# A hand-ordered attention and softplus-MLP kernel: a new order of all steps, a start without filler transposes, wider products in seven sweeps, and another DRAM layout for parked activations

## The chip, the cores and the metric

The kernel runs on one core of one Trainium2 chip. The metric is the device time of one execution in microseconds (us), as the median of several runs. One further execution was recorded by the hardware profiler; all rows below come from it.

## The reference

```python
def _attn_ref(x, state):                      # x: 8,8,512,64   state: 8,8,32,64
    scores = scale * x @ state^T ; a = softmax(scores) ; xread = a @ state
    scores2 = scale * state @ x^T ; a2 = softmax(scores2) ; sread = a2 @ x
    return concat([xread, sread], axis=2)     # 8,8,544,64
...
def _moe_ref(x, w_in, w_out):                 # x: 4352 x 512 after the heads are merged
    h = x @ w_in                              # 512 -> 2048
    g = max(h, 0) + log1p(exp(-abs(h)))       # softplus
    return (g @ w_out).astype(float32)        # 2048 -> 512
```

The weights arrive in double precision and are converted on the chip. Every large float32 product is made of three products of rounded halves (high by high, high by low, low by high): `PASSES`.

## The kernel before, in words

The eight batches are worked on as stages of one long list. For batch b, `B.Q` makes the scores (bank `sc`), a softmax follows on VectorE and ScalarE, `B.V` multiplies the state with the first weight (`V.b.c.g`), and `h.b.f` (16 of them per batch, six matmuls of 512 columns each) gives a 128-wide slice of the hidden layer in one PSUM bank. ScalarE takes the softplus (`s.b...`, line 719 or 646). `B.K` makes the same first-weight products for batches 4 to 7 together, parked in DRAM (`vd`). `B.R` and `T` make the read of x by the state (`rp`, `tp`); they need `Lx` and `Le` loads from DRAM (`in_xn`, `te`).

Batch 0 takes its second product in the plain form (`m.0.f.c`, bank `acc`, 12 matmuls of 512 columns for each f). Batches 1 to 7 park the softplus of each pair u of slices in DRAM (`Td.b.u`, tile `td`, 512 KB) and fetch it again for each half of the rows (`Tr.b.s.u`, 256 KB). The second product then runs in sweeps z = b.s, and one sweep 8.0 for the state rows: for each of 8 units u, VectorE forms sums and differences of four blocks (`sfa`, `sfb`, `sfc`, lines 744 to 747), ScalarE and VectorE split them into high and low halves (`gh`, `gl`, lines 312 and 328), and TensorE makes seven products of 256 columns in place of eight (a Winograd form). They collect in four banks X, Y, Z and Q over the sweep: steps `p.z.u.0` to `p.z.u.3`. A sweep ends with `e1` to `e6`, additions on VectorE (line 773) and one copy on ScalarE (line 776), which empty the banks into `ev`, and the stores `So`.

A product is three matmuls of 256 columns (line 766): low and high halves of the weight are two right-hand sides. Product 6 (bank Q) is in the wide form: the high half of g meets both halves of the weight in one matmul of 512 columns (line 762), the low half of g meets the high half of the weight in one of 256 (line 763). The bank then holds two parts, and the sweep's end adds both (`e6l`, `e6`). The last sweep, 7.1, has five banks and no wide product.

The order is written out by hand: `PLAN` is one list of steps, `name:engine:places`. The letter is T for TensorE, V and W for VectorE, A and C for ScalarE, S for the SyncE (SP) queue that issues the DMAs. C and W are the other way to convert a weight, with a plain copy (line 365) in place of the one on line 363 and two VectorE operations for one. The numbers behind a name are places in SBUF or PSUM; a step waits for the last user of its place. Each engine works through its steps in the order of the list, so a step that waits holds up all that stand behind it on its engine. Steps `w.i` are fillers: two 128x128 transposes into a bank that nobody reads (`wp`).

Of the kernel before, what the change touches and what calls it, by code (L numbers as in the profile page):

```python
# [56 lines left out]
Lk.0:S:23 Nm.1.1:V: D.1.0:T:5 cfa.0:V:24 Lk.1:S: cfa.1:V:25 m.0.2.2:T: cfb.0:V: cfb.1:V: wh.3:A:26 vl.1.0.1:V: gh.0.3:A:28 wl.3:V: Wh.0:A: Wh.1:A: gl.0.3:V:
ah.1.0:A:42 Wl.0:V: ah.0.0:A:32 w.4:T:2 w.5:T:2 w.6:T:2 w.7:T:2 w.8:T:2 w.9:T:2 w.10:T:2 w.11:T:2 m.0.3.3:T: Wl.1:V: ah.0.1:A:34 al.1.0:V: D.1.1:T:2 Lo.4:S:38
ch.2.1:C:87 cu.1.0:V:30 m.0.3.1:T: cu.1.1:V: ah.1.1:A:44 E.0.1:V: m.0.3.0:T: o.0.0.3:A:58 m.0.3.2:T: al.1.1:V: o.0.0.1:A:22 ch.2.0:C:93 Lo.5:S:74 cr.1.0:V:
h.1.0:T:1 o.0.0.0:A:67 cu.1.3:V:54 Li.3.0:S:46 cr.1.1:V: o.0.0.2:A:66 h.1.2:T:4 ch.2.2:C:95 cr.1.3:V: Sf.1.0:S: uh.0.2:A:36 cu.1.2:V: Li.3.1:S:78 al.0.0:V:  # L60
# [900 lines left out]
```

## Time and profile before

| what | value |
|---|---|
| median of 3 runs | 630.94 us (630.7 to 631.95) |
| the profiled execution's own time | 633.1 us |
| its span, first to last instruction | 631.3 us |
| TensorE, VectorE, ScalarE busy | 98%, 80%, 63% |
| DMA, mean rate over the span | 223 GB/s |

Matmuls are pipelined: a matmul's shown duration is longer than the distance to the next one, so the pace of a series is read from the starts, and a TensorE that is shown busy can still be idle for a moment. Idle time that the timeline prints in brackets is a gap that no modelled end covers, with what ended it.

### The profile page before, as it was taken

Reading aid. Unit: us, or ns where it says so; the run is one execution under the profiler, and the core shown is the slowest. Engines: PE = TensorE matmul, PEld = TensorE weight load, DVE = VectorE, ACT = ScalarE, POOL = GpSimd, SP = SyncE. Lnnn points to the kernel's source line nnn. Section 1 sums busy time; section 2 is a strip of 40 time slices with the busy share of each in tenths; the row PEclk is TensorE's granted clock in tenths of the full one; section 3 lists DMA queues with packets and bytes.
Section 4 is the critical chain, followed back from the end, with each engine's and each line's share of the span. In section 5 each row is a group of like instructions: output and inputs, shape, how many; then the busy total and the mean of one; then the engine's idle time right before and its main releaser. Section 6 shows DMA issues by size and latency. Waiting matters only on the chain.

```text
span 631.3 us, 12414 instructions
## 1 busy us (share of the span) xinstructions
PE 617.0 (98%) x4604; PEld 530.2 (84%) x4604; DVE 504.0 (80%) x1081; ACT 397.2 (63%) x659; POOL 1.0 (0%) x7
## 2 busy tenths in 40 slices
PE   8999999999999999999999999999999999999997
PEld 5576766577889988888988899899999999999997
DVE  3899688678999679885969988897975877878973
ACT  3899689999955448583736664576643454546440
POOL 0000000000000000000000000000000000000000
PEclk9999999999999999999999999999999999999999
DMA  9969766669906669968799857863848574431411
GB/s 343 415 226 327 289 232 240 255 231 399 353 19 216 193 200 254 294 206 281 241 294 319 255 189 257 266 224 124 288 128 271 208 246 141 138 107 33 152 51 35
DMA packets 64253, 141.07 MB, mean 223 GB/s; under 512 B 7360, under 2 KB 17600, under 8 KB 64192
## 3 DMA queue, kind: packets, MB, share of 16 engines
q1 hardware_dynamic: 63904, 139.62, 65.6%
q8 instruction: 36, 0.59, 0.4%
q10 hardware_dynamic: 288, 0.66, 0.3%
q14 instruction: 25, 0.20, 0.1%
HBM read 83.10 MB, written 57.15 MB: 222 GB/s over the span
## 4 chain that ended last, share of the span: by engine, by line
PE 70%; DVE 14%; DMA 10%; issue 2%; ACT 2%; SPq 2%; DVEq 0%; ACTq 0%
PE h L331 21%; PE pk_X L766 9%; PE pk_Y L766 9%; PE pk_Z L766 9%; PE acc L331 7%; DVE arena L328 4%; DMA arena<-td 3%; PE pk_Q L762 3%; PE h L820 2%; PE vp L331 2%; DMA arena<-vd 2%; PE vq L331 2%; SPq L319 1%; DVE arena L744 1%; PE pk_Q L763 1%
## 5 line engine op out<-in xcount | busy, mean ns | idle before, releaser
L312 ACT CAST arena<-arena 128x512 fp32r<-128x512 f32 (+2 forms) x255 | 185.8, 763 | 140.2 <-DVE arena L747 46.5
L328 DVE TENSOR_TENSOR arena<-arena,arena 128x512 fp32r<-128x512 f32 (+2 forms) x255 | 213.5, 858 | 58.3 <-ACT arena L312 56.1
L331 PE MATMUL h<-arena,arena 128*128 128x512 f32 x760 | 190.3, 399 | 0.0
L331 PEld LDWEIGHTS h<-arena,arena 128*128 128x128 f32 x760 | 138.3, 188 | 40.0 <-issue 4.2
L766 PE MATMUL pk_Y<-arena,arena 128*128 128x256 f32 x720 | 106.2, 284 | 0.4 <-DVE arena L328 0.4
L766 PE MATMUL pk_X<-arena,arena 128*128 128x256 f32 x720 | 105.5, 283 | 0.0
L766 PE MATMUL pk_Z<-arena,arena 128*128 128x256 f32 x696 | 103.8, 284 | 0.4 <-DVE arena L328 0.4
L766 PEld LDWEIGHTS pk_X<-arena,arena 128*128 128x128 f32 x720 | 96.6, 189 | 5.9
L766 PEld LDWEIGHTS pk_Y<-arena,arena 128*128 128x128 f32 x720 | 94.9, 190 | 1.1 <-DVE arena L328 0.6
L766 PEld LDWEIGHTS pk_Z<-arena,arena 128*128 128x128 f32 x696 | 92.2, 191 | 1.8 <-issue 0.8
L719 ACT ACTIVATE arena<-h 128x512 f32<-128x512 f32 x112 | 66.6, 613 | 29.8 <-PE h L331 25.7
L744 DVE TENSOR_TENSOR arena<-arena 128x256 f32<-128x256 f32 x120 | 49.5, 419 | 25.0 <-DMA arena<-td 23.9
L331 PE MATMUL acc<-arena,arena 128*128 128x512 f32 x192 | 45.7, 396 | 0.0
L762 PE MATMUL pk_Q<-arena,arena 128*128 128x512 f32 x112 | 44.8, 401 | 0.0
L331 PEld LDWEIGHTS acc<-arena,arena 128*128 128x128 f32 x192 | 35.8, 188 | 8.1 <-issue 1.0
L747 DVE TENSOR_TENSOR arena<-arena 128x128 f32<-128x128 f32 x120 | 33.6, 287 | 1.7
L746 DVE TENSOR_TENSOR arena<-arena 128x128 f32<-128x128 f32 x120 | 33.4, 287 | 1.4
L763 PE MATMUL pk_Q<-arena,arena 128*128 128x256 f32 x112 | 31.4, 280 | 0.0
L820 PE MATMUL h<-sreadT,arena 128*128 128x512 f32 x64 | 22.8, 393 | 0.0
L762 PEld LDWEIGHTS pk_Q<-arena,arena 128*128 128x128 f32 x112 | 21.3, 190 | 1.3 <-issue 0.8
L378 DVE SCALAR_TENSOR_TENSOR arena<-arena,arena 128x512 int32<-128x512 int32 x31 | 21.0, 688 | 0.5
L763 PEld LDWEIGHTS pk_Q<-arena,arena 128*128 128x128 f32 x112 | 21.3, 190 | 0.0
(99 smaller groups left out, 548.2 us busy)
## 6 DMA issues: line engine op xcount, KB each, us to landing
td<-arena SPq DMA_DIRECT2D x56, 512.0 KB, 4.3
arena<-td SPq DMA_DIRECT2D x112, 256.0 KB, 4.4
arena<-in_w_in_dram SPq DMA_DIRECT2D x16, 512.0 KB, 8.6
arena<-in_w_out_dram SPq DMA_DIRECT2D x16, 512.0 KB, 7.5
vd<-arena SPq DMA_DIRECT2D x32, 256.0 KB, 2.9
arena<-vd SPq DMA_DIRECT2D x64, 128.0 KB, 4.3
arena<-in_xn_dram SPq DMA_DIRECT2D x16, 512.0 KB, 6.4
arena<-in_xt_dram SPq DMA_DIRECT2D x15, 512.0 KB, 6.5
```

What stands on the lines that cost most here:

```text
L312: nc.scalar.copy(dst, src)
L328: lambda e: eng(e).tensor_tensor(r(dlo()), src(), dhi(), ALU.subtract))
L331: nc.tensor.matmul(dst, lhs, rhs, start=start, stop=stop)
L378: nc.vector.scalar_tensor_tensor(u, h2().bitcast(I32), 3, u, ALU.logical_shift_left, ALU.bitwise_or)
L719: nc.scalar.activation(t[:, :, 0::3] if i == 0 else t[:, :, 1:3], src.rearrange("p (s c t) -> p s c t", s=2, t=P), AF.Softplus)
L744: op(f"sfa.{k}", "V", t, [f"t.{k}:a"], lambda e, g=blocks: nc.vector.tensor_tensor(g()[:, 0:2], g()[:, 4:7:2], g()[:, 7:8].broadcast_to([P ...
L746: op(f"sfb.{k}", "V", [t[0], f"t.{k}:a"], [f"t.{k}:b"], lambda e, g=blocks: nc.vector.tensor_tensor(g()[:, 2], g()[:, 1], g()[:, 4], ALU.add))
L747: op(f"sfc.{k}", "V", [t[1], f"t.{k}:b"], [f"t.{k}:c"], lambda e, g=blocks: nc.vector.tensor_tensor(g()[:, 3], g()[:, 5], g()[:, 2], ALU.s ...
L762: nc.tensor.matmul(at(bank), g(0), r(wform(u, m)(slice(0, 2))), start=first, stop=False, skip_group_check=True)
L763: nc.tensor.matmul(at(bank)[:, 0:256], g(1), r(wform(u, m)(0)), start=False, stop=True, skip_group_check=True)
L766: nc.tensor.matmul(at(bank)[:, 256 * half:256 * half + 256], g(gi), r(wform(u, m)(wi)), start=first and pi == ps[0] and i == 0, stop=i == ...
L820: nc.tensor.matmul(hb, r(w[:, 0, cs]), r(at("sreadT")[:, :, kt, :]), start=kt == 0, stop=False, skip_group_check=True)
```

## The change

Four things, made together.

- `WIDE` names seven sweeps (4.1, 5.0, 5.1, 6.0, 6.1, 7.0 and 8.0) in which products 4, 5 and 6 take the wide form. Products 4 and 5 (bank Z before) then need a bank each, Z and W, so that a unit has five steps (`p.z.u.4` is new) and the sweep five banks; its end has four additions of 256 columns (`e5l`, `e5`, `e7l`, `e7`) in place of one of 512 (`e5`).
- Of the 14 filler steps, `w.1` to `w.13` are gone. `ch.o3` and `cu.o3`, and two more pairs, move from one conversion form to the other.
- The order of all steps is new. TensorE's own order is nearly the same up to the sweeps; moved are mainly `B.R0` to `B.R3`, `B.Q6`, `B.Q7`, the `T` steps and some `h` steps. VectorE's, ScalarE's and SP's orders, and many places, are new throughout.
- `td` is two solid blocks for each pair of slices, one for each half of the rows; the store writes two runs of 2 KB per partition in place of one of 4 KB, and a fetch reads one solid block of 256 KB.

In the token that guards the overwriting of half of a weight (`used`), the name is new and the steps it stands for are the same.

```diff
-WIDE = {}
+WIDE = {(4, 1): (4, 5, 6), (5, 0): (4, 5, 6), (5, 1): (4, 5, 6), (6, 0): (4, 5, 6), (6, 1): (4, 5, 6), (7, 0): (4, 5, 6), (8, 0): (4, 5, 6)}
...
-            used = [f"acc.{b}.{x}.{c}:{f1}" for b, x, f0, fe in RUNS if f0 <= f1 < fe for c in range(4)]
+            used = [f"W.{f1}:u{b}{c}" for b in PLAIN for c in range(4)]
...
-            op(f"m.{k}.{c}", "T", [...], [f"{acc}:{f}"], gemm2)
+            op(f"m.{k}.{c}", "T", [...], [f"{acc}:{f}", f"W.{f}:u{b}{c}"], gemm2)
...
-            store(f"Td.{b}.{u}", [...], lambda b=b, u=u: io.td[b, u], lambda b=b, u=u: at(f"tt.{b}.{u}"), [f"D:td.{b}.{u}"])
+            store(f"Td.{b}.{u}", [...], lambda b=b, u=u: io.td[b, u].rearrange("s p n -> p s n"), lambda b=b, u=u: at(f"tt.{b}.{u}").rearrange("p (s n) -> p s n", s=2), [f"D:td.{b}.{u}"])
...
-                     lambda b=b, s=s, u=u: io.td[b, u][:, 512 * s:512 * s + 512], [f"D:td.{b}.{u}"])
+                     lambda b=b, s=s, u=u: io.td[b, u][s], [f"D:td.{b}.{u}"])
...
-    io.td = {(b, u): dp.tile([P, 1024], F32, ...) ...}
+    io.td = {(b, u): dp.tile([2, P, 512], F32, ...) ...}
```

TensorE's order at the places that the prediction speaks of (unchanged neighbours cut):

```diff
-V.0.0.1.0 w.2 w.3 V.0.0.1.1 B.V1.0
+V.0.0.1.0 V.0.0.1.1 B.V1.0
...
-D.1.0 m.0.2.2 w.4 w.5 w.6 w.7 w.8 w.9 w.10 w.11 m.0.3.3 D.1.1 m.0.3.1 m.0.3.0 m.0.3.2 h.1.0
+D.1.0 m.0.2.2 m.0.3.3 D.1.1 m.0.3.1 m.0.3.0 m.0.3.2 h.1.0
...
-p.2.0.0.0 p.2.0.0.1 B.R4 h.4.12 p.2.0.0.2
+p.2.0.0.0 p.2.0.0.1 p.2.0.0.2 B.R4 p.2.0.1.1
...
-p.2.0.3.2 B.R0 p.2.0.3.3
+p.2.0.3.2 p.2.0.3.3 p.2.0.4.1 p.2.0.4.2 p.2.0.4.3 p.2.0.5.1 p.2.0.4.0 p.2.0.5.0 p.2.0.5.2 B.R0
...
-p.2.1.1.3 B.R1 h.5.3
+p.2.1.1.3 h.5.3 B.R1
...
-p.3.0.0.2 p.3.0.0.3 p.3.0.1.0 p.3.0.1.1 p.3.0.1.2 p.3.0.1.3 h.5.9 p.3.0.2.0 B.R2
+p.3.0.0.2 B.R2 p.3.0.0.3
...
-p.3.0.3.3 h.5.10 B.Q6 h.5.11 p.3.0.4.0
+p.3.0.3.3 h.5.10 h.5.11 p.3.0.4.1 p.3.0.4.2 p.3.0.4.0 B.Q6
...
-B.R3 h.5.15 T.3 T.5
+B.R3 p.3.1.4.2 T.3
```

ScalarE's and VectorE's order in the start, and SP's ahead of `Lz.3` and around `Le.2` and `Lz.6`:

```diff
-A: wh.2 ch.o3 m.1.0 m.1.1 ch.1.0 ch.1.1 ch.1.2 ch.1.3 s.0.3 wh.3 gh.0.3 Wh.0 Wh.1 ah.1.0
+A: wh.2 ch.o3 s.0.3 m.1.0 m.1.1 gh.0.3 wh.3 ch.1.0 ch.1.1 ah.1.0
-V: N.1.0 N.1.1 Nm.1.0 Nm.1.1 cfa.0 cfa.1 cfb.0 cfb.1 vl.1.0.1 wl.3 gl.0.3 Wl.0 Wl.1 al.1.0 cu.1.0 cu.1.1 E.0.1 al.1.1
+V: N.1.0 vl.1.0.1 Nm.1.0 gl.0.3 wl.3 N.1.1 Nm.1.1 cu.1.0 cu.1.1 al.1.0 cr.1.0 al.1.1
-S: Td.1.0 Sf.2.0 Td.1.1 Sf.2.1 Td.1.2 Lt.2.0 Lt.2.1 Lt.3.0 Lt.3.1 Td.1.3 Lz.2 Sf.3.0 Lz.3
+S: Lo.5 Lo.6 Sf.2.0 Sf.2.1 Lt.2.0 Lt.2.1 Lt.3.0 Lt.3.1 Td.1.2 Td.1.3 Lz.2 Td.1.0 Td.1.1 Sf.3.0 Sf.3.1 Lz.3
...
-S: Tr.3.0.2 Tr.3.0.3 Lx.2.0 Lx.2.1 Td.5.3 Le.2.0 Le.2.1 Le.2.2 Le.2.3
+S: Lx.2.0 Lx.2.1 Le.2.0 Le.2.1 Le.2.2 Le.2.3 Tr.3.0.2 Td.5.3 Tr.3.0.3
...
-S: So.2.1.0 Lt.6.0 So.2.1.1 Tr.3.0.4 Tr.3.0.5 Lt.6.1 Td.5.4 Tr.3.0.7 Lz.6
+S: So.2.1.0 Lz.6 So.2.1.1 Tr.3.0.6 Tr.3.0.4 Se.5.0 Se.5.1 Lq.3.1 Tr.3.0.5 Lt.6.0 Td.5.4 Lt.6.1 Lq.3.0 Tr.3.0.7
```

## Rows read from the trace of the kernel before

**Rows 1.** Page, part 1: busy time, share of the span, instructions of each engine.
```profile
PE 617.0 (98%) x4604; PEld 530.2 (84%) x4604; DVE 504.0 (80%) x1081; ACT 397.2 (63%) x659; POOL 1.0 (0%) x7
```
**Rows 2.** Busy time by stretch; the last three columns: granted clock, DMA share, GB/s.
```profile
20.00:44.00 24.00, 23.53 (x125) 14.90 (x124) 20.93 (x44) 21.44 (x38) 0.00 (x0) 1.00 0.84 325
44.00:100.00 56.00, 55.38 (x367) 37.68 (x366) 46.67 (x94) 48.41 (x87) 0.00 (x0) 1.00 0.77 275
...
240.00:360.00 120.00, 114.70 (x1134) 104.39 (x1133) 99.95 (x233) 76.61 (x119) 0.00 (x0) 1.00 0.87 271
...
430.00:620.00 190.00, 190.00 (x1429) 179.76 (x1428) 148.80 (x312) 91.53 (x147) 0.00 (x0) 1.00 0.47 153
```
**Rows 3.** Timeline of TensorE between 240 and 430: pieces with an idle gap.
```profile
253.41 1.10 PE L331 MATMUL rp<-arena,arena 128*32 128x64 f32 x64 [1.54 <-DMA td<-arena]
265.97 1.10 PE L331 MATMUL rp<-arena,arena 128*32 128x64 f32 x64 [0.21 <-issue]
281.39 0.74 PE L766 MATMUL pk_Y<-arena,arena 128*128 128x256 f32 x4 [0.37 <-DVE arena L328]
291.35 1.10 PE L331 MATMUL rp<-arena,arena 128*32 128x64 f32 x64 [1.01 <-DMA out_dram<-arena]
332.33 1.09 PE L331 MATMUL sc<-arena,arena 64*32 64x512 f32 x16 [2.06 <-DMA arena<-in_zp_dram]
361.41 0.44 PE L539 MATMUL tp<-ident,arena 128*128 128x128 f32 x2 [0.50 <-ACT arena L536]
```
**Rows 4.** Timeline of TensorE in the start: fillers and their neighbours.
```profile
22.32 0.94 PE L615 MATMUL wp<-ident 128*128 128x128 f32 x4
...
37.21 3.85 PE L615 MATMUL wp<-ident 128*128 128x128 f32 x16
40.82 0.94 PE L331 MATMUL acc<-arena,arena 128*128 128x512 f32 x3
```
**Rows 5.** Timeline of ScalarE in the start.
```profile
23.87 0.37 ACT L312 COPY arena<-vp 128x256 f32<-128x256 f32 x1 [0.66 <-PE vp L331]
...
30.02 1.28 ACT L363 ACT_TABLE_LOAD   x1
...
35.25 1.28 ACT L646 ACT_TABLE_LOAD   x1
```
**Rows 6.** Timeline of VectorE in the start.
```profile
36.22 0.76 DVE L595 SCALAR_TENSOR_TENSOR arena<-arena,arena 128x256 f32<-128x256 f32 x2
...
41.30 0.68 DVE L480 TENSOR_REDUCE nm<-arena 128x1 f32<-128x512 f32 x1
42.85 0.69 DVE L328 TENSOR_TENSOR arena<-ab,arena 128x512 fp32r<-128x512 f32 x1 [0.68 <-ACT arena L312]
```
**Rows 7.** Timeline of TensorE: three narrow products, then products in the wide form.
```profile
621.05 0.52 PE L766 MATMUL pk_W<-arena,arena 128*128 128x256 f32 x3
621.41 0.52 PE L766 MATMUL pk_Q<-arena,arena 128*128 128x256 f32 x3
...
525.12 0.40 PE L820 MATMUL h<-sreadT,arena 128*128 128x512 f32 x1
525.36 0.28 PE L821 MATMUL h<-sreadT,arena 128*128 128x256 f32 x1
525.47 0.39 PE L820 MATMUL h<-sreadT,arena 128*128 128x512 f32 x1
```
**Rows 8.** Timeline of VectorE at the end of sweep 8.0.
```profile
606.21 0.42 DVE L773 TENSOR_TENSOR arena<-pk_X,arena 128x256 f32<-128x256 f32 x1
...
608.00 0.68 DVE L773 TENSOR_TENSOR arena<-pk_Z,arena 128x512 f32<-128x512 f32 x1
608.60 0.41 DVE L773 TENSOR_TENSOR arena<-pk_Q,arena 128x256 f32<-128x256 f32 x1
608.93 1.08 DVE L328 TENSOR_TENSOR arena<-arena,arena 128x896 fp32r<-128x896 f32 x1
```
**Rows 9.** Page, part 6: DMA issues, KB each, us from issue to landing.
```profile
td<-arena SPq DMA_DIRECT2D x56, 512.0 KB, 4.3
```

More of the change, by code (lines that the diff above doesn't have):

```diff
@@ L57 @@
[L57 to L60, printed above, removed]
@@ L261 @@
[L261 to L264 removed]
+Lt.0.0:S:16 Lt.0.1:S:18 Lz.0:S:20 Li.0.0:S:22 Li.0.1:S:24 Lz.1:S:21 Lt.1.0:S:26 Lt.1.1:S:28 Lo.0:S:30 Lo.1:S:32 Li.0.2:S:34 B.Q0:T:0,1 Li.0.3:S:36 qk.0.0.0:A:38
@@ new lines @@
+Li.3.2:S:56 vh.1.1.0:A:38 Li.3.3:S:46 vh.1.1.1:A:66 vl.1.1.0:V: Lo.5:S:76 vh.0.1.0:A:82 Lo.6:S:88 vl.1.1.1:V: h.1.3:T:0 vh.0.1.1:A:48 vl.0.1.0:V: ch.2.0:A:62
+vl.0.1.1:V: ch.2.1:A:65 h.1.5:T:6 E.0.1:V: ch.2.2:A:52 ch.2.3:A:53 cu.2.0:V:96 h.1.4:T:5 cu.2.1:V: uh.0.2:A:54 cr.2.0:V: s.1.0.0:A:58 cr.2.1:V: h.1.6:T:1
+cu.2.2:V:92 Sf.2.0:S: cu.2.3:V: cr.2.2:V: s.1.2.1:A:80 h.1.7:T:4 cr.2.3:V: s.1.2.0:A: ul.0.2:V: Sf.2.1:S: s.1.3.0:A:86 cfa.0:V:62 Lt.2.0:S:22 kh:A:18
+B.V0.2+V1.2:T:2,6,5,1 cfb.0:V: Lt.2.1:S:70 s.1.3.1:A: kl:V: Lt.3.0:S:72 ch.3.0:C:65 cfc.0:V: Lt.3.1:S:52 ch.3.1:C:94 cfd.0:V: Td.1.2:S: cu.3.0:W:38 ch.3.2:C:66
@@ new lines @@
+Sv.0.1.1:S: D.2.0:V:70 s.0.12:A:71 h.0.14:T:1 Td.1.7:S: D.2.1:V:72 ah.2.0:A:24 M.3.1:V: ah.2.1:A:42 h.0.15:T:3 Lt.4.0:S:62 al.2.0:V: s.0.13:A:73 Lt.4.1:S:80
+s.0.14:A:8 al.2.1:V: uh.2.1:A:58 Ms.3.0:V: B.K0.0:T:5,7 s.0.15:A:70 ul.2.1:V: m.3.0:A: B.V2.0+V3.0:T:4,6,2,0 Ms.3.1:V: cfa.1:V:72 cfb.1:V: cfc.1:V:
+cv.0.0.0:A:56 B.K0.3:T:1,3 Lz.4:S:57 N.3.0:V: vh.2.0.1:A:22 Sv.0.0.0:S: vh.2.0.0:A:44 vl.2.0.1:V: vh.3.0.0:A:20 vl.2.0.0:V: vh.3.0.1:A:30 B.K0.2:T:5,6
+cv.0.0.1:A:36 vl.3.0.0:V: h.2.0:T:4 cv.0.3.0:A:37 Sv.0.0.1:S: vl.3.0.1:V: cv.0.3.1:A:56 Sv.0.3.0:S: Nm.3.0:V: m.3.1:A: Sv.0.3.1:S: h.2.1:T:7 cfd.1:V:
@@ new lines @@
+h.2.11:T:7 cv.1.3.1:A:79 Sv.1.3.0:S: s.2.5.0:A:92 Sv.1.3.1:S: B.K2.2:T:2,1 ch.o5:C:6 s.2.5.1:A: cu.o5:W:4 Lo.9:S:44 B.K3.0:T:6,4 cv.2.2.0:A:10 Td.2.5:S:
+cr.o5:V: B.K2.3:T:3,0 cv.2.2.1:A:11 Sv.2.2.0:S: cv.3.0.0:A:80 D.4.0:V:81 Sv.2.2.1:S: h.3.9:T:5 cv.3.0.1:A:6 Sv.3.0.0:S: cfa.2:V:61 cv.2.3.0:A:35 Sv.3.0.1:S:
+cv.2.3.1:A:79 Sv.2.3.0:S: h.3.10:T:7 wh.4:A:76 Sv.2.3.1:S: gh.0.6:A:58 wl.4:V: ch.o6:C:26 B.K3.3:T:2,1 gl.0.6:V: wh.5:A:40 cu.o6:W:27 Lo.10:S:2 B.K3.2:T:6,4
+s.3.4.1:A:0 wl.5:V: cv.3.3.0:A:65 h.3.8:T:3 cv.3.2.0:A:10 cr.o6:V: Sv.3.3.0:S: cv.3.2.1:A:11 cfb.2:V: Sv.3.2.0:S: cv.3.3.1:A:26 cfc.2:V: h.3.11:T:0 Lo.7:S:92
@@ new lines @@
+s.3.6.0:A:42 h.3.15:T:2 Lo.13:S:18 cu.o7:W:11 s.3.6.1:A: Lo.14:S:62 cr.o11:V: s.3.7.0:A:20 m.0.4.0:T:6 m.4.1:A: cr.o7:V: Td.2.6:S: m.0.4.1:T:1 Td.2.7:S:
+cfa.3:V:26 cfa.4:V:49 Td.3.6:S: m.0.4.2:T:7 cfb.3:V: wh.11:A:36 cfb.4:V: m.0.4.3:T:4 N.4.1:V: gh.0.11:A:92 m.0.5.0:T: gh.0.9:A:38 gl.0.11:V: m.0.5.1:T:
+ch.o12:A:65 wl.11:V: wh.7:A:50 m.0.5.2:T: gl.0.9:V: s.3.7.1:A: m.0.5.3:T: cu.o12:V:54 Lo.15:S:82 wl.7:V: m.0.6.0:T: cr.o12:V: m.0.6.1:T: ch.o13:C:55 Td.3.7:S:
+Nm.4.1:V: m.0.6.2:T: wh.12:A:96 Tr.1.0.0:S:34 cu.o13:W:65 m.0.6.3:T: gh.0.12:A:56 wl.12:V: ch.o14:C:5 m.0.7.0:T: gl.0.12:V: vh.4.0.0:A:18 m.0.7.1:T: Th.2:A:58
@@ new lines @@
+p.1.0.0.1:T:0 So.0.2:S: So.0.3:S: p.1.0.0.2:T:5 p.1.0.0.3:T:2 p.1.0.1.0:T: gh.1.0.2:A:12 p.1.0.1.1:T: gl.1.0.2:V: p.1.0.1.2:T: Tr.1.0.6:S:86 p.1.0.1.3:T:
+sfa.1.0.4:V: h.4.0:T:6 Lv.4.1.0:S:82 sfa.1.0.5:V: gh.1.0.3:A:4 sfb.1.0.4:V: Lv.4.1.1:S: sfb.1.0.5:V: sfc.1.0.4:V: Lv.4.1.2:S: sfc.1.0.5:V: gl.1.0.3:V: h.4.1:T:1
+Lv.4.1.3:S: s.4.0.0:A:94 cfa.5:V:55 cfb.5:V: p.1.0.2.0:T: cfc.5:V: s.4.0.1:A: p.1.0.2.1:T: sfa.1.0.6:V: cfd.5:V: Th.5:A:60 Td.4.0:S: p.1.0.2.2:T: sfb.1.0.6:V:
+Eh.5:A: sfc.1.0.6:V: Tl.5:V: Wh.5:A: p.1.0.2.3:T: p.1.0.3.0:T: El.5:V: Tr.1.0.7:S:28 gh.1.0.4:A:12 Wl.5:V: p.1.0.3.1:T: cfa.6:V:70 gh.1.0.5:A:8 cfb.6:V:
@@ new lines @@
+p.1.0.3.2:T: gl.1.0.4:V: Tr.1.1.0:S:80 Wh.6:A: p.1.0.3.3:T: h.4.2:T:7 gl.1.0.5:V: vh.4.1.0:A:94 gh.1.0.6:A:4 cfc.6:V: Wl.6:V: h.4.3:T:4 Tr.1.1.1:S:26
+vh.4.1.1:A:48 cfd.6:V: Th.6:A:54 gl.1.0.6:V: p.1.0.4.0:T: s.4.1.0:A:18 Tl.6:V: p.1.0.4.1:T: Eh.6:A:38 sfa.1.1.0:V: s.4.1.1:A: El.6:V: p.1.0.4.2:T: sfb.1.1.0:V:
+sfa.1.0.7:V: Td.4.1:S: sfc.1.1.0:V: p.1.0.4.3:T: sfb.1.0.7:V: vl.4.1.0:V: p.1.0.5.0:T: gh.1.1.0:A:12 sfc.1.0.7:V: p.1.0.5.1:T: vl.4.1.1:V: Tr.1.1.2:S:86
+gl.1.1.0:V: p.1.0.5.2:T: p.1.0.5.3:T: sfa.1.1.1:V: h.4.4:T:6 gh.1.0.7:A:8 cfa.7:V:79 sfb.1.1.1:V: cfb.7:V: sfc.1.1.1:V: Wh.7:A: gl.1.0.7:V: h.4.5:T:1
```

418 lines of the change are left out of this document (201 added, 217 removed).

## The prediction

> **What bounds the kernel now.** I read the page first: TensorE is busy for 617.0 of 631.3 us, VectorE for 504.0, ScalarE for 397.2 [rows 1]. So TensorE sets the end, and an edit is worth what it takes from TensorE's work or from the moments in which TensorE waits. The rows by stretch show where it waits: from 430 to 620 not at all (190.00 of 190), from 240 to 360 for 5.30 us (114.70 of 120), with DMA at 0.87 of its engines, and from 20 to 100 for little that shows; there, fillers stand in the gaps [rows 2]. TensorE's timeline names the waits of the middle: 1.54, 0.21 and 1.01 us ahead of three `rp` groups (steps `B.R4`, `B.R0`, `B.R1`, whose operands come by DMA), 2.06 ahead of `sc` (`B.Q6`, for the load `Lz.6`), 0.37 for VectorE's split and 0.50 for `X.3` ahead of `T.3` [rows 3]. Four of the six are for loads, 4.82 us of 5.69 in all. In the start, 16 filler transposes fill 37.21 to 40.82, and four stand at 22.32 [rows 4]. The granted clock is 1.00, its upper level of 2.4 GHz, in each of these stretches [rows 2].
>
> **The start.** `w.2` and `w.3` take 0.94 us of TensorE's order [rows 4]. Behind them ScalarE waits 0.66 us for the `vp` product [rows 5]. The fillers are read by nobody, so the product can come earlier by the smaller of the two, about 0.6.
>
> `w.4` to `w.11` stand from 37.21 to 40.82, 3.61 us [rows 4]. Their removal is worth that only if what TensorE needs next (`m.0.3.3`, `D.1.1`, then `h.1.0`, which needs `al.1.1`) comes earlier too, so I count the queue of VectorE between `N.1.0` and `al.1.1`. Taken out of it: two pairs `cfa`, `cfb` of 0.76 each, 1.5 (one row shows a pair, the other is alike) [rows 6]; `Wl.0` and `Wl.1`, two of 256 columns at the 0.33 between starts that such an addition shows (608.60 to 608.93) [rows 8], 0.7; and `E.0.1`, with the idle time behind it, 41.30 to 42.85, 1.55 [rows 6]. Put in: `cr.1.0`, 512 columns, 0.60 (608.00 to 608.60) [rows 8]. That makes 3.1 less. On ScalarE, `ch.o3` changes to the plain copy and `s.0.3` moves ahead of `m.1.0`: the tables loaded at 30.02 and 35.25, 1.28 us each, become one [rows 5], and four conversions no longer stand ahead of `s.0.3`. The second VectorE operation that the plain copy needs, some 0.35, I leave within the rounding. The shortest of 3.61 and 3.1 counts: 3.1. `w.1`, `w.12` and `w.13` I take at nothing; from 0 to 0.7.
>
> The start so gains 3.7, bounds 0.6 (VectorE or a load in the place of the fillers) and 4.5.
>
> Against it stands SP's queue. Ahead of `Lz.3`, which `B.Q2+Q3` needs, now stand `Lo.5`, `Lo.6` and `Sf.3.1` as well, three times 512 KB, 1.57 MB; at the 275 GB/s of 44 to 100 that is 5.7 us of transfers [rows 2], partly in a stretch where the queue had room (share 0.77). Bounds are 0 and the whole 3.7. I take 0.5, since the start's gain comes from work that other engines are also rid of.
>
> **The wide products.** Three matmuls of 256 columns take 0.36 us (621.05 to 621.41); a pair of 512 and 256 takes 0.35 (525.12 to 525.47) [rows 7]. The columns are the same 768; only one matmul's overhead goes. Two more products, 8 units, 7 sweeps: 112 products by 0.01, about 1.0 us; bounds 0 and 2, from the rounding. One weight load in three goes with them: 112 of 4604.
>
> The Trainium skill ("TensorE: Matmul & The Clock Gate", "LDWEIGHTS (loading the stationary operand)" and "The mechanism" of its Part 3) says that a weight load takes its columns over 1.2 GHz, 107 ns for 128, and overlaps running matmuls only in another row group. By that rule the 112 loads would be worth 12 us. The pace of 0.12 us per 256 columns leaves no room for it: 107 ns of columns and 107 of weights would be 0.21 [rows 7].
>
> On VectorE each of the seven sweeps ends with four additions of 256 columns, 0.33 apart, in place of one of 512, 0.60: 0.73 more, 5.1 in all [rows 8]. From 430 to 620 VectorE has 41 us idle of 190, which hides it [rows 2]. Without that cover it costs at the borders of sweeps, because two neighbouring sweeps now want ten banks of eight: the fourth and fifth step of the new sweep wait until X and Y of the old one are empty. By the rows the additions run from 606.21, and Y is empty by 608.0 [rows 8], 1.8 us; the new sweep's first three steps (0.72, 0.72 and 0.35) last as long, and the old sweep's steps behind its last X as long again. A split of 1.08 that gets ahead [rows 8] still fits, a second does not. I take 0.2 for each border, 1.4; bounds 0 and 1.6 each, 11.
>
> **The middle.** By TensorE's pace a step of six matmuls of 256 columns lasts 0.72 (six by 0.12), one of `h` 1.4 (six by the 0.24 between 525.12 and 525.36) [rows 7]. `B.Q6` moves behind four more steps, 3.5 us, and its late load `Lz.6` from behind `Lt.6.1`, `Td.5.4` and three `Tr` in SP's queue to ahead of them; `Lt.6.1`, which it needs too, goes behind `Td.5.4`, with 3.5 us to make that good: 2.06 to 0. `B.R0` moves behind nine more: 0.21 to 0. `B.R1` moves behind `h.5.3`, 1.4, and the transposes that feed it (`H.1`) come sooner on VectorE: 1.01 to 0. `B.R4` moves behind one step, 0.72: 1.54 to 0.8. `B.R2`, which had no idle time, moves forward by seven steps, 5.0 us (four sixfold ones, two `p` of 0.36, one `h`); its loads move ahead of `Tr.3.0.2`, `Td.5.3` and `Tr.3.0.3`, 1 MB or 3.9 us at 271 GB/s [rows 2]. It may wait up to 1.1, I take 0.5. `T.3` now has 0.72 of work between it and `B.R3` where 1.4 stood, so its 0.50 stays, and so does VectorE's 0.37. So 5.30 us become 2.2: 3.1 gained. Bounds: all 5.3, and nothing, if DMA sets the pace there; its share of 0.87 is near that.
>
> **The parked activations.** `Td` moves the same 512 KB in runs of half the length, 56 times [rows 9]; no row shows what a run costs. Between a store and its fetch lie many steps, so even a landing one whole 4.3 us later is waited for by nobody. Bounds 0 and those 4.3 for one store that is fetched soon; I take 0.
>
> **Sum.** 631.3 - 3.7 + 0.5 - 1.0 - 3.1 + 1.4 = 625.4 us of span. The profiled execution took 633.1 outside its span; the median of the runs is 630.94, so the same 5.9 off it gives **625.0**.
>
> **Rivals.**
>
> *DMA keeps the pace of the middle.* The share of 0.87 over 120 us speaks for it [rows 2]; against it, most waits have a load that was only issued late. Then a start that is 3.7 sooner is waited for again and the moved reads still come late: what stays is 1.0 and a part of the rest, 628 to 630.5, some 629.
>
> *The borders of sweeps* (slower). It sits at seven borders, where additions of a sweep of five banks run 0.73 longer. If two splits get ahead there, TensorE waits up to 1.6 at each: 11.2 in place of 1.4, so 634.8. It turns the gain into a loss from 1.0 us per border on. Against it, TensorE waited for no border between 430 and 620 [rows 2].
>
> *All waits of the middle go and the borders are free.* 5.3 in place of 3.1, no 1.4, no 0.5: 620.9, and 619 with the upper bounds of the start.
>
> *The fillers hold the clock.* Without them TensorE waits in the start where it had transposes to run; should its clock fall to 1.2 GHz there, the products behind would take double, some 2 to 4 us as the stretch 37.21 to 40.82 is long, and the start gains nothing: 629 to 632. The rows show 1.00 [rows 2], with work in each gap, so they cannot exclude it. The Trainium skill's page named above says ("Why this matters for your kernels") that idle gaps between bursts send the clock back to half; no row here shows an idle gap long enough to see it happen.
>
> *Weight loads are paid in full.* Each of the 112 that go is then worth as much as 256 columns, 0.12 us, the most that a pace of 0.12 could hide: 13 us in place of 1.0, so 613. The equal paces of rows 7 speak against it. The rule of the skill told above would make it so.
>
> **How the numbers follow.** Forecast, 621.5 to 628: 0.53. DMA: 0.20. Borders: 0.12. No waits: 0.08. Clock: 0.05. Weight loads: 0.02. Less than 0.2% (1.3 us) can't be told from no change. Faster: 0.53, the 0.10 of no waits and weight loads, two thirds of DMA: 0.76; same: 0.08, from DMA and clock; slower: 0.16, from borders, clock and the rest. Leaving out the weight loads, half of no waits and most of the borders gives 618.5 to 632.5.
>
> **What would show it.** The first long `h` series behind `acc` some 3.7 earlier, and no `wp` but one pair; an idle gap ahead of the next `sc` of 32 would mean the 0.5 is too small. From 240 to 360 TensorE idle for about 2 us, none ahead of `B.Q6`. Pairs of 512 and 256 in `pk_Z` and `pk_W` 0.35 apart. Gaps ahead of a sweep's fourth or fifth step, released by line 773, would show the borders. VectorE busy some 5 us more. The prediction is wrong if a load that was in time before is now late, at a step that I did not name.

## The result, and the profile after

The changed kernel takes 623.46 us (median of 4 runs, 622.8 to 624.58), the kernel before, beside it, 630.82 (4 runs, 628.75 to 631.95): a ratio of 0.989 with a 95% interval from 0.9869 to 0.9911. The forecast was 625.0 in a range from 618.5 to 632.5. The profiled execution took 624.01 us, its span is 622.2.

Page, part 1, of the changed kernel, to hold against [rows 1]:

```profile
PE 611.6 (98%) x4466; PEld 522.1 (84%) x4466; DVE 508.9 (82%) x1104; ACT 395.9 (64%) x655; POOL 1.0 (0%) x7
```

TensorE does 138 instructions less (112 by the wide products, 26 by the thirteen fillers), VectorE is busy 4.9 us longer, as forecast. Busy time by stretch, after (columns as in [rows 2]):

```profile
20.00:44.00 24.00, 23.42 (x149) 15.80 (x149) 21.43 (x43) 19.01 (x34) 0.00 (x0) 1.00 0.99 362
44.00:100.00 56.00, 54.73 (x361) 36.97 (x361) 47.44 (x96) 53.08 (x95) 0.00 (x0) 1.00 0.75 274
240.00:360.00 120.00, 117.75 (x1150) 107.29 (x1149) 101.49 (x237) 76.44 (x121) 0.00 (x0) 0.99 0.87 275
360.00:430.00 70.00, 70.00 (x532) 63.36 (x531) 58.94 (x131) 45.91 (x67) 0.00 (x0) 1.00 0.70 221
430.00:612.00 182.00, 182.00 (x1285) 167.94 (x1284) 148.38 (x325) 84.53 (x134) 0.00 (x0) 1.00 0.47 154
```

and of the kernel before the stretch that rows 2 left out, with the piece in it that has an idle gap:

```profile
360.00:430.00 70.00, 69.01 (x538) 62.59 (x538) 59.20 (x135) 44.46 (x67) 0.00 (x0) 1.00 0.72 234
```
```profile
424.81 0.74 PE L766 MATMUL pk_Z<-arena,arena 128*128 128x256 f32 x4 [0.45 <-DVE arena L328]
```

This wait is for the split `gl.4.1.4` (line 328; in the kernel before, `p.4.1.4.2` is the step that needs it). VectorE's timelines, before and then after, show what the two orders put ahead of that split:

```profile
421.26 0.43 DVE L744 TENSOR_TENSOR arena<-arena 128x256 f32<-128x256 f32 x1 [0.43 <-DMA arena<-td]
...
422.68 0.43 DVE L744 TENSOR_TENSOR arena<-arena 128x256 f32<-128x256 f32 x1 [0.19 <-DMA arena<-td]
423.14 0.29 DVE L746 TENSOR_TENSOR arena<-arena 128x128 f32<-128x128 f32 x1
423.47 0.29 DVE L747 TENSOR_TENSOR arena<-arena 128x128 f32<-128x128 f32 x1
423.68 2.08 DVE L328 TENSOR_TENSOR arena<-arena,arena 128x896 fp32r<-128x896 f32 x2
```
```profile
412.99 0.29 DVE L752 TENSOR_TENSOR arena<-arena 128x128 f32<-128x128 f32 x1
...
414.33 1.09 DVE L333 TENSOR_TENSOR arena<-arena,arena 128x896 fp32r<-128x896 f32 x1 [0.79 <-ACT arena L317]
```

In the old order the sums of units 5 and 6 stand there (`sfa.4.1.5` and `sfa.4.1.6`, the two lines that wait for a fetch from `td`); in the new one they come behind `gl.4.1.4`.

From 240 to 360 the idle time is 2.25 us where it was 5.30; from 360 to 612 TensorE shows no wait. The six gaps of [rows 3] are gone, and one new gap stands in their place, with TensorE's clock behind it at its lower level. TensorE's timeline after, then the granted clock of two stretches (the column before the last two):

```profile
331.89 0.47 PE L771 MATMUL pk_Y<-arena,arena 128*128 128x256 f32 x2
334.51 1.22 PE L771 MATMUL pk_Y<-arena,arena 128*128 128x256 f32 x4 [2.15 <-DVE arena L333]
335.53 1.48 PE L771 MATMUL pk_Z<-arena,arena 128*128 128x256 f32 x6
336.81 0.63 PE L767 MATMUL pk_Q<-arena,arena 128*128 128x512 f32 x1
337.24 0.41 PE L768 MATMUL pk_Q<-arena,arena 128*128 128x256 f32 x1
337.45 0.77 PE L771 MATMUL pk_X<-arena,arena 128*128 128x256 f32 x4
```
```profile
326.00:332.00 6.00, 6.00 (x55) 1.00 0.96 292
334.00:337.00 3.00, 2.49 (x11) 0.55 0.89 283
```

The step is `p.3.0.7.1`, the first of its unit in the order. Two matmuls run on `gh`, the third needs `gl.3.0.7`. VectorE's timeline shows what stands ahead of that split (line 333):

```profile
327.53 0.43 DVE L749 TENSOR_TENSOR arena<-arena 128x256 f32<-128x256 f32 x1 [1.54 <-DMA arena<-td]
327.87 1.31 DVE L443 STREAM_TRANSPOSE arena<-sc 128x512 f32<-128x512 f32 x2
329.10 0.25 DVE L751 TENSOR_TENSOR arena<-arena 128x128 f32<-128x128 f32 x1
...
332.18 0.68 DVE L459 TENSOR_TENSOR arena<-arena,mx 128x512 f32<-128x512 f32 x1
332.78 0.70 DVE L528 STREAM_TRANSPOSE arena<-arena 128x512 f32<-128x512 f32 x1
333.41 1.05 DVE L333 TENSOR_TENSOR arena<-arena,arena 128x896 fp32r<-128x896 f32 x1
```

The fetch `Tr.3.0.7` is late (1.54 idle ahead of `sfa.3.0.7`), and then batch 6's scores (`A.6.0`, `A.6.1`, the operations to `Ms.6.0`) and `H.3.0` go ahead of the split in VectorE's order.

In the start `w.0` is the only filler left. From 20 to 62 us, where it showed no wait before, TensorE now shows two, ahead of `D.1.1` for the last step of a softmax (`Nm`, line 469) and ahead of `h.1.9` for a split (line 333):

```profile
35.78 0.66 PE L430 MATMUL ab<-ident,arena 128*128 128x128 f32 x4 [0.43 <-DVE arena L469]
36.20 2.30 PE L336 MATMUL acc<-arena,arena 128*128 128x512 f32 x9
38.34 1.98 PE L336 MATMUL h<-arena,arena 128*128 128x512 f32 x8
...
55.64 4.62 PE L336 MATMUL h<-arena,arena 128*128 128x512 f32 x19 [0.70 <-DVE arena L333]
```

`h.1.0` starts at 38.34 where it started at 44.12. Starts of steps, read from TensorE's timelines of four kernels (two are experiments, below), put the shift into places:

| start of, us | before | old_no_fillers | changed | new_fillers |
|---|---|---|---|---|
| `w.0` (first filler) | 8.38 | 7.20 | 7.41 | 7.28 |
| `h.1.0` | 44.12 | 39.25 | 38.34 | 42.18 |
| `p.1.0.0.0` (first sweep) | 192.31 | 187.46 | 187.16 | 191.02 |
| `p.2.0.0.0` | 250.28 | 245.42 | 245.12 | 248.98 |
| `p.4.0.0.0` | 381.56 | 375.31 | 374.21 | 376.45 |
| span | 631.3 | 627.7 | 622.2 | 624.4 |
| from `p.4.0.0.0` to the span's end | 249.75 | 252.39 | 247.99 | 247.99 |

About 1.0 of the spans' 9.1 lies ahead of `w.0` and belongs to that one execution: in every other profile `w.0` starts between 7.1 and 7.5. The four parts of the rest: from `w.0` to `p.1.0.0.0` 4.18 less, on to `p.2.0.0.0` nothing (57.96 in all fourteen profiles), on to `p.4.0.0.0` 2.19 less, and from there to the end 1.76 less. This last stretch takes 247.99 in each of the nine profiles that have the changed kernel's orders there and its wide products, and 249.75 to 252.39 in the four with the old order.

### The profile page after: what moved, and what is told of

Its sections match the earlier page's. It is cut to its first block, busy times and chain, and to the rows that moved or that the text cites. A ratio compares the mean times of both kernels' runs of the same rounds, so it can differ in the third digit from the quotient of the medians.

```text
span 622.2 us, 12168 instructions
## 1 busy us (share of the span) xinstructions
PE 611.6 (98%) x4466; PEld 522.1 (84%) x4466; DVE 508.9 (82%) x1104; ACT 395.9 (64%) x655; POOL 1.0 (0%) x7
## 4 chain that ended last, share of the span: by engine, by line
PE 81%; DVE 9%; DMA 5%; ACT 2%; issue 2%; SPq 0%; DVEq 0%; ACTq 0%
PE h L336 23%; PE pk_Y L771 12%; PE pk_X L771 12%; PE acc L336 6%; PE pk_Z L771 6%; PE pk_Q L767 4%; DVE arena L333 2%; PE h L825 2%; PE pk_W L767 2%; PE pk_Z L767 2%; PE pk_Q L768 2%; DMA td<-arena 2%; PE vq L336 2%; PE vp L336 2%; PE h L826 1%
## 5 line engine op out<-in xcount | busy, mean ns | idle before, releaser
L333 DVE TENSOR_TENSOR arena<-arena,arena 128x896 fp32r<-128x896 f32 (+2 forms) x255 | 212.8, 856 | 54.0 <-ACT arena L317 52.5
L771 PE MATMUL pk_Z<-arena,arena 128*128 128x256 f32 x360 | 54.4, 286 | 0.0
L771 PEld LDWEIGHTS pk_Z<-arena,arena 128*128 128x128 f32 x360 | 48.4, 193 | 1.1 <-issue 0.8
L767 PEld LDWEIGHTS pk_Q<-arena,arena 128*128 128x128 f32 x112 | 21.4, 191 | 3.9 <-issue 0.8
L767 PE MATMUL pk_W<-arena,arena 128*128 128x512 f32 x56 | 22.7, 405 | 0.0
L767 PE MATMUL pk_Z<-arena,arena 128*128 128x512 f32 x56 | 22.2, 397 | 0.0
```

The costliest lines, as they stand in the source:

```text
L333: lambda e: eng(e).tensor_tensor(r(dlo()), src(), dhi(), ALU.subtract))
L767: nc.tensor.matmul(at(bank), g(0), r(wform(u, m)(slice(0, 2))), start=first, stop=False, skip_group_check=True)
L771: nc.tensor.matmul(at(bank)[:, 256 * half:256 * half + 256], g(gi), r(wform(u, m)(wi)), start=first and pi == ps[0] and i == 0, stop=i == ...
```

## The experiments

"Before" in the ratios is the kernel before, run beside each on the same chip; the changed kernel's ratio is 0.989.

**narrow.** Products 4 and 5 again of three matmuls each, in the same steps and banks.

```diff
-                        if pi in wide:
+                        if pi in wide and pi == 6:
...
-PLAN: e5l.4.1 e7l.4.1 ... e5l.8.0 e7l.8.0   (fourteen additions)
```

> The changed kernel with products 4 and 5 again as three matmuls of 256 columns, in the same five steps, banks and order; the fourteen additions e5l and e7l go with them. My theory (only one matmul's overhead goes with each wide pair): TensorE's work grows by 0.95 us, what the two traces differ by there, so the kernel is 0.5 to 1.5 us slower than the changed one, about 624.5. Rival, weight loads paid in full: 112 more of 0.12, about 13 us slower, 636. Rival, the borders of the sweeps cost something in the changed kernel (VectorE's additions run longer there): with fourteen additions fewer it is as fast or faster, 622 to 623.5.

Measured: 0.9894 (0.9869 to 0.992). From `p.4.0.0.0` to the span's end 248.83 us (375.94 to 624.77), in the changed kernel 247.99: 0.84 for 112 products, 7.5 ns each. By the ratios it is 0.3 slower than the changed kernel, which cannot tell 0.84 from nothing but excludes the 13 us of a full weight load for each. A price of the borders is not there either: from `p.5.0.0.0` to `p.5.1.0.0` it is 29.73 in this kernel, whose sweep 5.0 has five banks, and 29.73 in the kernel before, whose sweep has four; with the wide products and the additions `e5l` and `e7l` it is 29.59. TensorE is busy 182.00 of 182 from 430 to 612 in both kernels of the new order.

**old_no_fillers** and **new_fillers.** The fillers by themselves: taken out of the old order, put back into the new.

```diff
-PLAN (before): w.1:T:3 w.2:T:2 w.3:T:2 w.4:T:2 ... w.11:T:2 w.12:T:4 w.13:T:4
+PLAN (changed): V.0.0.1.0 w.2:T:2 w.3:T:2 ... m.0.2.2 w.4:T:2 ... w.11:T:2
```

> The kernel before, without its fillers w.1 to w.13, nothing else changed. My theory (the prediction's: the start gains the shorter of what TensorE and what VectorE is rid of): VectorE's old order holds al.1.1 back, so the fillers stood in time that TensorE waits in any case; 0 to 1 us faster, about 630.3, with idle time of some 3 us in their place. Rival, the fillers themselves were the start's price: 3 to 4.5 us faster, 626.5 to 628. Rival, the fillers held the clock: it is slower than before by 1 us or more, with a granted clock below 1 in the stretch from 30 to 50.

> The changed kernel with ten fillers put back at the old kernel's places: w.2 and w.3 behind V.0.0.1.0, w.4 to w.11 behind m.0.2.2. My theory (the start gained from both, the fillers and a shorter queue of VectorE): TensorE is now the later of the two, so all of the fillers' time comes back at its steps: 4.5 us by their 0.45 each, less what idle time the changed kernel has there (about 0.5); 3.5 to 4.5 us slower than the changed kernel, about 627.5. Rival, VectorE or a load would hold the start anyway: 0 to 1.5 us slower. Rival, the fillers hold the clock: faster than the changed kernel.

Measured: from `w.0` to `p.1.0.0.0` it is 183.93 us before (183.45 and 183.46 in two further kernels with the old start), 180.26 without fillers, 179.75 in the changed kernel, 183.74 with ten fillers put back. So in the start the thirteen fillers are worth 3.2 in the old order (183.46 to 180.26) and ten of them 4.0 in the new; without fillers the new order is 0.5 shorter. My theory for `old_no_fillers` fell: VectorE's old queue did not hold `al.1.1` back enough to matter. The clock rival fell too; without fillers the granted clock of the start stays 1.00, here in `old_no_fillers`:

```profile
20.00:44.00 24.00, 22.85 (x135) 15.74 (x142) 22.92 (x49) 23.93 (x44) 0.00 (x0) 1.00 0.92 350
44.00:100.00 56.00, 55.07 (x387) 36.30 (x369) 47.06 (x94) 48.78 (x86) 0.00 (x0) 1.00 0.77 282
```

In the old order the end does not get all of it: `old_no_fillers` has 0.9983 (0.9961 to 1.0004), by the ratio 1.1 us under the kernel before, between 2.5 faster and 0.3 slower, which excludes the start's 3.2. Its profile shows where the gain goes: `B.Q6` still waits 2.19 for `Lz.6`, with the clock at its lower level behind it, and from `p.4.0.0.0` to the end it takes 252.39 where the kernel before takes 249.75, with gaps of 0.78, 1.49 (at `p.4.1.4.2`) and 0.39 where that has 0.45. `new_fillers` has 0.9927 (0.9907 to 0.9946), 2.3 us over the changed kernel; the two intervals together make that about 0.5 to 4, so how much of the 4.0 arrives in the new order is not shown. In one pair of profiles all of it does: again (below) is as long in the middle (127.49 and 127.47), and its span, counted from `w.0`, is 4.0 shorter.

**old_lz6.** One late load of the kernel before, moved alone.

```diff
-S: Lt.6.0 So.2.1.1 Tr.3.0.4 Tr.3.0.5 Lt.6.1 Td.5.4 Tr.3.0.7 Lz.6
+S: Lz.6 Lt.6.0 So.2.1.1 Tr.3.0.4 Tr.3.0.5 Lt.6.1 Td.5.4 Tr.3.0.7
```

> The kernel before with one load moved: Lz.6 goes ahead of Lt.6.0 in SP's queue, five loads and stores earlier. The prediction's step (each wait of the middle is worth its own length): the 2.06 us ahead of B.Q6 go, 2 us faster, 628.9. Rival, the DMA sets the pace there: the wait goes at B.Q6 but stands again at Lt.6.1 or at the next late load, 0 to 0.7 us faster.

Measured: 1.0032 (1.0013 to 1.0051), 2.0 us slower. Its timeline has no gap ahead of `sc` any more, and this one 10 us later, for the split of a fetch behind `Lz.6` in the queue (`gl.3.0.6`):

```profile
338.24 0.74 PE L764 MATMUL pk_X<-arena,arena 128*128 128x256 f32 x4 [1.28 <-DVE arena L326]
```

So a wait of the middle that goes is not a gain of its length. The rival had said 0 to 0.7 faster; slower it had not foreseen.

**early_split.** The cause of the new gap, mended.

```diff
-V: sfa.3.0.7 A.6.0 A.6.1 sfb.3.0.7 E.3.0 sfc.3.0.7 sfa.3.1.0 M.6.1 sfb.3.1.0 M.6.0 sfc.3.1.0 Ms.6.0 H.3.0 gl.3.0.7
+V: A.6.0 A.6.1 sfa.3.0.7 sfb.3.0.7 sfc.3.0.7 E.3.0 sfa.3.1.0 gl.3.0.7 M.6.1 sfb.3.1.0 M.6.0 sfc.3.1.0 Ms.6.0 H.3.0
-A: qk.6.1 e.3.0 gh.3.0.7
+A: qk.6.1 gh.3.0.7 e.3.0
```

> The changed kernel with the splitting of unit 3.0.7 ahead of other work: A.6.0 and A.6.1 in VectorE's idle time ahead of sfa.3.0.7, then sfb and sfc at once, gh.3.0.7 on ScalarE ahead of e.3.0, gl.3.0.7 ahead of M.6.1. My theory: the 2.15 us of idle time ahead of p.3.0.7.1 is only the place of gl.3.0.7 in VectorE's queue, and the granted clock falls to its lower level behind it because of it; gl.3.0.7 then ends near 330.7, 1.2 us before the product can start, so both the 2.15 and the 1.6 us of double length go: 3.8 us in the profiled execution, 2 to 3.8 over the runs, about 620.5. Rival, the idle time moves on to the next split (gl.3.1.0, m.6.0 or the late loads): 0 to 1 us, the idle time stands at p.3.1.0.3. Rival, the clock falls there for another reason than the wait: the 2.15 go, the clock of the stretch from 330 to 340 stays below 1, about 621.5.

Measured: 0.9862 (0.9841 to 0.9884), 622.61 us: by the ratios 1.8 under the changed kernel, with intervals that overlap, where the theory had 2 to 3.8; that it is faster is not shown. The gap is gone and the clock stays 1.00, but the profiled execution (at 625.74 the longest of the five) waits elsewhere, at reads (`rp`) that the changed kernel's profile does not wait for, and behind the mended place:

```profile
269.03 1.10 PE L336 MATMUL rp<-arena,arena 128*32 128x64 f32 x64 [1.98 <-DMA arena<-vd]
...
313.07 1.10 PE L336 MATMUL rp<-arena,arena 128*32 128x64 f32 x64 [0.66 <-DMA arena<-td]
338.95 0.39 PE L768 MATMUL pk_Q<-arena,arena 128*128 128x256 f32 x1 [1.01 <-DVE arena L333]
```

**again** and **light_stores.** The changed kernel once more, and with less DMA in the middle (most columns of the output rows of batches 1 to 3 are not stored).

```diff
-                    store(f"So.{z}.{i}", ..., io.out[row:row + P], at(ev)[:, 512 * i:512 * i + 512])
+                    store(f"So.{z}.{i}", ..., io.out[row:row + P, 0:n], at(ev)[:, 512 * i:512 * i + n])   # n = 64 for b in 1, 2, 3
```

> The changed kernel itself, once more, beside the others of this call: ratio to the kernel before 0.989 by its first four runs, 0.987 to 0.991. Its waits of the middle stand elsewhere than in its first profile if they belong to the execution and not to the order: ahead of B.R0 or B.R2 as well as ahead of p.3.0.7.2; those of the start (h.1.9 0.97, h.2.0 1.07) are the same to 0.05 us in either case.

> The changed kernel with the output stores of the batches 1 to 3 cut to their first 64 of 512 columns, so that most of those rows of the output are left out; nobody in the kernel waits for these stores. Eight of them fall into the stretch from 240 to 360: 1.8 MB less of 33 MB, some 6.7 us of transfers at the 275 GB/s of that stretch. Theory, the DMA sets the pace of the middle (the waits of 4 to 7 us there stand at another step in each execution, since each goes to whichever load is late): the waits in that stretch fall by 2 to 4 us, so does the time, about 620.5. Rival, the middle's waits are each a matter of its own place in the order: 0 to 0.7 us, about 623.

Measured: again 0.989 (0.9854 to 0.9926), runs from 622.52 to 629.99; its profile waits at `B.R4` and, shorter, at the same split:

```profile
248.68 1.21 PE L336 MATMUL rp<-arena,arena 128*32 128x64 f32 x64 [1.13 <-DMA td<-arena]
334.75 0.74 PE L771 MATMUL pk_Y<-arena,arena 128*128 128x256 f32 x4 [1.55 <-DVE arena L333]
```

The waits for reads belong to the execution, then; that at `p.3.0.7.1` to the order: it is 1.55 to 2.15 in all six profiles with the changed kernel's order there (the changed kernel twice, narrow, new_fillers, light_stores, old_td), and absent from all four with early_split's. light_stores has 0.9881 (0.9857 to 0.9905): 1.8 MB less from 240 to 360 gave by the ratios 0.6 us, nothing that can be told, where the theory had 2 to 4. Its profile waits 2.14 at `p.3.0.7.1`.

**early_light.** Both together.

> early_split and light_stores together (the output stores of batches 1 to 3 cut to 64 of 512 columns, the rest of those rows left out). Each alone took one of two causes away and left the other: early_split had 1 to 2 us of waits for loads, light_stores 3 us ahead of p.3.0.7.2. Theory, two causes in series (a late load, and behind it VectorE's order), each of which hides what the other would give: together they give more than the sum of the two, 3 to 5 us faster than the changed kernel, about 619.5. Rival, the volume of DMA is no cause: no more than early_split alone, 621.7.

Measured: 0.9831 (0.9807 to 0.9856), 622.29 us, runs from 621.74 to 622.71; beside it, again had a median of 625.19. It is 3.7 under the changed kernel by the ratios, with an interval that does not meet that of the result, against 1.8 and 0.6 for its parts, though the intervals allow a plain sum too. No read waits for a load from 240 to 345; `B.R3` at 356 does, 0.67. This fits two causes in series, the late load and VectorE's order behind it, and a spread of the runs that comes from the late loads (1.0 us here, 7.5 in again); neither is shown.

**old_td** and **old_new_td.** The layout of the parked activations: the old one in the changed kernel, the new one in the kernel before.

```diff
-    io.td = {(b, u): dp.tile([2, P, 512], ...)}     # old_td; old_new_td is the same edit the other way
+    io.td = {(b, u): dp.tile([P, 1024], ...)}
```

> The changed kernel with the old layout of the parked activations: rows of 1024, stored in one run and fetched by halves. The prediction took the layout at nothing: 0, about 623.5. Rival, the fetch of a solid block is worth something in the middle, since its landing took 3.8 us in place of 4.4 and VectorE waited 7.0 us in all for such fetches in place of 23.9: 1 to 3 us slower than the changed kernel, the waits of the middle longer. Rival, the shorter runs of the store cost more than the fetch gains: faster by up to 1.

> The kernel before with the new layout of the parked activations alone: solid blocks of 512 columns for each half. Prediction: 0. Rival by old_td (0.8 us slower with the old layout, interval -1 to 2.6): 0.5 to 1.5 us faster than the kernel before, the fetch landing in 3.8 in place of 4.4 us.

Measured: old_td 0.9903 (0.9876 to 0.993), 0.8 us slower than the changed kernel by the ratios, not to be told from nothing; old_new_td 0.9973 (0.9949 to 0.9997), 1.7 us faster than the kernel before (0.2 to 3.2), which is only just clear of nothing. Landing of the fetch (the last figure, the median in us) on the page, old_new_td, then old_td; the kernel before has 4.4, the changed kernel 3.8:

```profile
arena<-td SPq DMA_DIRECT2D x112, 256.0 KB, 4.0
```
```profile
arena<-td SPq DMA_DIRECT2D x112, 256.0 KB, 4.2
```

From `p.2.0.0.0` to `p.4.0.0.0` the four profiles with the old layout took 131.28, 131.75, 129.89 (old order) and 130.62 us (new order); with the new layout 127.95 (old order), 129.09 and 127.49 (the changed kernel twice), and from 127.5 to 131.1 in the other seven. The two ranges overlap: that the layout is worth something there is likely by these numbers and not shown, and a gain by the new order of the reads does not show at equal layout.

**combo** and **best.** Two attempts at more.

```diff
-T: h.0.6 h.1.9 ... h.0.4:T:4 h.0.5
+T: h.0.6 h.0.4:T:0 h.1.9 ... h.0.5                       # combo, with early_split; s.0.4 behind s.0.6
...
-V: cu.3.0 cu.3.1 vl.1.2.0 vl.1.2.1 ... M.6.1 sfb.3.1.0 M.6.0 sfc.3.1.0 Ms.6.0 ... vl.5.3.0 sfb.3.1.1 vl.5.3.1 sfc.3.1.1
+V: cu.3.0 vl.1.2.0 vl.1.2.1 cu.3.1 ... sfb.3.1.0 sfc.3.1.0 ... vl.5.3.0 vl.5.3.1 sfb.3.1.1 sfc.3.1.1 M.6.1 M.6.0 Ms.6.0   # best, with early_split
-A: vh.0.2.0 vh.0.2.1 s.1.1.0 ... m.6.0 vh.5.3.0 vh.5.3.1
+A: s.1.1.0 vh.0.2.0 vh.0.2.1 ... vh.5.3.0 vh.5.3.1 m.6.0
```

> early_split and one edit of the start: h.0.4, whose operands are there, moves ahead of h.1.9, whose split is 0.97 us late in every execution so far. If a wait of the start is worth its length (nothing varies there from one execution to the next): h.1.9's wait goes and the steps behind are 0.9 to 1.0 sooner up to the middle. At the end, by the theory that the DMA paces the middle, 0.3 to 0.7 of it is left, about 0.5 faster than early_split, 621.5; if each wait is worth its length, 0.9 to 1.0, 621.

> early_split, with what it showed late next mended: vl.5.3.0 and vl.5.3.1 (1.30 us ahead of h.5.12 there) and sfb and sfc.3.1.1 go ahead of M.6.1, M.6.0 and Ms.6.0 on VectorE, m.6.0 behind vh.5.3.1 on ScalarE; and at the start vl.1.2.1 goes ahead of cu.3.1, s.1.1.0 ahead of vh.0.2.0. If waits of VectorE's order are worth their length: h.1.9 starts 0.5 sooner, 1.0 to 1.3 go at h.5.12, so 1.5 to 1.8 faster than early_split, about 620.2. Rival, each is given back at the next late load, as in old_lz6: within 0.7 of early_split, 621.7.

Measured: combo 0.9935 (0.9912 to 0.9957). I gave `h.0.4` a bank that `s.1.1.1` still reads, so TensorE waits 3.32 us there, and `s.0.4` a place that held `ow.1`, so part of the second weight has other values; it says nothing on its question. best 0.9887 (0.9864 to 0.991), by the ratios 1.6 slower than early_split, with intervals that overlap: counted from `w.0`, `h.1.9` starts 0.3 sooner, but `h.0.4` then waits for `s.0.6` and starts 1.0 later than in the changed kernel, and behind `h.5.12` the split of the next unit is late:

```profile
342.31 0.58 PE L768 MATMUL pk_Q<-arena,arena 128*128 128x256 f32 x1 [1.42 <-DVE arena L333]
```

The theory (1.5 to 1.8 faster) fell. The rival (within 0.7 of early_split) has the better part: waits of VectorE's order that go there come back at a later step.

## Why the prediction came out, step by step

The time was right within its range; how it came about was forecast only in part. The forecast of each part beside what the two profiles of the result show:

| part | forecast, us | profiles |
|---|---|---|
| ahead of `w.0` (that one execution) | none | 0.97 faster |
| the start, less the price in SP's queue | 3.2 faster | 4.18 faster |
| the middle, `p.2.0.0.0` to `p.4.0.0.0` | 3.1 faster | 2.19 faster |
| wide products | 1.0 faster | 0.84 faster (narrow) |
| borders of sweeps | 1.4 slower | nothing |
| waits behind `p.4.0.0.0` | not seen | 0.9 faster |
| sum | 5.9 faster | 9.1 faster, of the medians 7.4 |

That the sum came near is in part luck: the middle, priced 0.9 too high by this pair of profiles, stands against the start, the borders and the stretch behind `p.4.0.0.0`, priced too low. The middle's 2.19 is itself one draw of several (below).

- **The start** (3.7 forecast): 3.7 to 4.2 measured from `w.0` to the first sweep. The size holds, the way to it does not: I let VectorE's queue set it (3.1, "the shortest of 3.61 and 3.1"), but without any change of VectorE's order the fillers give 3.2, and the orders 0.5. The 3.1 also counts the 0.68 of [rows 6] in which VectorE only waits for ScalarE as work that goes with `E.0.1`. The 0.5 for SP's queue ahead of `Lz.3` did not come, `B.Q2+Q3` has no gap; `h.1.9` waits 0.70 for VectorE instead. And I counted the start in full at the end; in the old order it does not arrive in full (1.1 of 3.2 by the medians), in the new one that is open.
- **The wide products** (1.0): 0.84. The Trainium skill ("TensorE: Matmul & The Clock Gate", "The mechanism" of Part 3) says that a weight load overlaps running matmuls only where the row group differs, and in the same section that it is also pulled ahead into a background weight buffer. The 7.5 ns for a matmul and its load disagree with the first as it stands; they agree with the second, which the prediction left out.
- **The borders** (1.4 against): nothing; 29.73 with four banks and with five. No step behind `p.4.0.0.0` waits in any profile of the new order.
- **The middle** (3.1): the step that failed, though the size is near. The waits at `B.Q6`, `B.R0` and `B.R1` went as forecast, and B.R4's with them in this execution. But each was priced at its length in one execution, as if that length were gained. B.Q6's wait does belong to the order (1.08 to 2.19 in the three profiles that have `Lz.6` in its old place, none in the other eleven), yet old_lz6 shows that taking it away alone gains nothing. Those of the reads come and go. The changed kernel waits at none of the reads in one profile and 1.13 at `B.R4` in the other, its variants at `B.R4`, `B.R0` or `B.R2` by turns, and the same kernel takes 129.09 and 127.49 there. At equal layout the new order does not show as shorter. The term's sum is also on two bases: `T.3`'s 0.50 stands at 361.41, outside the 5.30 of 240 to 360; on one base the same terms make 3.5.
- **The layout** (0): the second that failed. I asked only who waits for a fetch that lands later; it lands earlier (3.8 against 4.4 us), in a stretch with many late loads, and was worth 1.7 (0.2 to 3.2) in the old order. In the new one nothing could be told.
- **Not seen**: the old order's wait for `gl.4.1.4`, at `p.4.1.4.2` (424.81). It is 0.45 of idle time there and 1.49, 1.60 and 1.29 in the three other kernels with the old order, where the sums of two more units, with the waits for their fetches, stand ahead of the split; none with the new order has it. From `p.4.0.0.0` to the end the four take 0.9 to 3.6 more than narrow (248.83). No run changes that order alone, so the cause and the price are read from timelines and not tested. And the new wait at `p.3.0.7.1`.

The rival "DMA keeps the pace of the middle" may have named the right resource (early_light), but did not count that the fetches land sooner after the change. What stays open: which of the late loads is the first, whether the new order of the reads is worth anything, and how the 7.4 of the medians divides, since the middle differs by up to 3.6 us between executions of nearly the same order.

## What to carry to other kernels

Profile the same kernel more than once before a wait is given a price: here the gaps that stood in every execution were a matter of an engine's or a queue's order, those that came and went were waits for loads, and a load that was moved ahead made another one late. Where an engine works through a fixed list, look for work on late loads that stands ahead of a result which is needed sooner (`gl.4.1.4`, `gl.3.0.7`). Fillers can cost most of their time (4.0 of the 4.5 us of ten, here in the new order); check what waits behind them, not whether they sit in a gap. The layout of a transfer that nobody seems to wait for may count.
